# Converting most of the weights in pieces of 768 and 384 columns instead of three of 384

## The chip, the cores and the metric

One core of a Trainium2 chip. The metric is the device time of one execution in microseconds (us); of the kernel before there are three runs, 700.78 to 702.23, median 701.29. The profiled execution is a run of its own, with a time of its own.

## The reference

An attention-like recurrence feeds a bilinear feed-forward block. For each batch and head, a 48x48 state is multiplied by a complex number per row and takes in an outer product; then the feed-forward block runs on all 3072 tokens:

```python
mag = np.sqrt(a_re * a_re + a_im * a_im)
scale = np.minimum(mag, 0.999) / (mag + 1e-06)
a_re_n, a_im_n = (a_re * scale, a_im * scale)
for t in range(S):                      # S = 768, B = 4, H = 8, D = 48
    new_re = ar * S_re - ai * S_im
    new_im = ar * S_im + ai * S_re
    S_re, S_im = (new_re + kv, new_im)  # kv = outer(k[t], v[t])
    y[:, :, t] = einsum(q[t], S_re)
...
a = x @ w_a                             # 3072x384 by 384x1536
b = x @ w_b
return (a * b @ w_out)                  # 1536x384
```

The weights come as 64-bit floats. The kernel makes 32-bit ones of their two words itself.

## The kernel before

**Units.** The tokens are worked in 12 units (`NU`): two batches at a time, 128 time steps each, so 256 tokens. For each unit there are three kinds of work. `prep(u)` on VectorE (DVE), with logarithms, exponentials and squares on ScalarE (ACT), forms the running products of `a` and multiplies them into `q` and `k` (lines 178 to 192 scale `a`, L210 to L293 are the products, L308 the multiplication into tile `qk`). `stack(u)` copies `qk` by ten DMAs on SyncE's queue (SP), L345, into tile `stk`, one or two DMAs per head; it needs the last L308 of that unit. `attn(u)` on TensorE (PE) forms scores from `stk` (L378, four heads to a PSUM tile `pm`); DVE masks each tile (L381, tile `am`), four of these per unit; PE forms outputs (L418, tile `xp`), which ACT copies in two parts to `xh` (L422) and, after one correcting matmul (L426), `xl` (L429).

**Feed-forward.** For each unit 12 blocks `f` of 128 rows of the inner dimension follow: `gemm1` (18 matmuls L481 into tile `ab`), the product of its halves on ACT and DVE (L489 to L492), `gemm2` (6 matmuls L499). All matmuls of the feed-forward take a number as a high and a low part, so each weight is needed as a pair.

**Weights.** A block has 1152 weight columns: 384 of `w_a`, 384 of `w_b`, 384 of `w_out`. `load_weights` fetches them in three pieces of 384 columns (L124, 36 DMAs). `split_weights` converts a piece: three DVE operations (L133, L135, L137) put the 32-bit number together in a scratch tile `o_sb`; ACT rounds it to the high part (L141); PE forms the number minus its high part (L146, a matmul in two passes, and L147); ACT copies that to the low part (L148). The scratch tile is free again when L141 and L146 have read it. There are three of them, in the pool `moe`; two are also used at each unit's end for the output. Piece `w13` in the listings is piece 1 of block 3.

**Order.** Each engine runs its instructions in one fixed order. A scheduler makes it at build time, by its own idea of durations and free buffers; the source gives only the sequence of statements and some priorities (`MOE_FIRST`, `ATTN_FIRST`). The source asks for the first unit's `prep`, then six blocks of conversion, then the first `attn`; the other six blocks are converted during the first unit's feed-forward, one per block. The main loop runs `attn` one unit ahead and `prep` two or three.

Of the kernel before, what the change touches and what calls it, by code (L numbers as in the profile page):

```python
# [8 lines left out]
F32 = mybir.dt.float32  # L9
# [14 lines left out]
NJ = 3  # L24
# [18 lines left out]
KS = 2 * D  # L43
LAG = 2
HB = 3
O_BUFS = 3
CONV_ON_AB = 7
NCHK = NU * G + NU + 1
WPART = ((0, DM), (DM, DM), (2 * DM, DM))
CONV_FIRST = 6  # L50
P1_AT = 4
MOE_FIRST = 4000
# [14 lines left out]
def tile_kernel(ctx: ExitStack, tc: tile.TileContext, a_d, qk_d, v_d, w_d, qn_d, kn_d, vn_d, an_d, out_d):  # L67
# [51 lines left out]
        return ap.bitcast(F32R)  # L119

    def load_weights(f):
        for m, (c0, n) in enumerate(WPART):
            raws[f, m] = wpool.tile([128, n, 2], U32, name=f"w{m}{f}")
            sync.dma_start(out=raws[f, m].rearrange("p c s -> p (c s)"),  # L124
                           in_=w_d[f, :, c0:c0 + n].bitcast(U32))

    def split_weights():
        for f in range(NF):
            for m, (c0, n) in enumerate(WPART):
                raw = raws[f, m]  # L130
                t = moe.tile([128, n], F32, name="o_sb", bufs=O_BUFS)
                tu = t.bitcast(U32)
                vec.tensor_scalar(out=tu, in0=raw[:, :, 1], scalar1=3, scalar2=0x3FFFFFFF,  # L133
                                  op0=ALU.logical_shift_left, op1=ALU.bitwise_and)
                vec.scalar_tensor_tensor(out=tu, in0=raw[:, :, 0], scalar=29, in1=tu,  # L135
                                         op0=ALU.logical_shift_right, op1=ALU.bitwise_or)
                vec.scalar_tensor_tensor(out=tu, in0=raw[:, :, 1], scalar=0xC0000000, in1=tu,  # L137
                                         op0=ALU.bitwise_and, op1=ALU.bitwise_or)
                w_t[f, m] = wpool.tile([128, 2, n], F32, name=f"w{m}{f}")
                hi, lo = w_t[f, m][:, 0], w_t[f, m][:, 1]  # L140
                act.copy(out=r(hi), in_=t)  # L141
                if f < CONV_ON_AB:
                    lp = ps_ab.tile([128, 512], F32, name="ab")
                else:
                    lp = ps_m.tile([128, 512], F32, name="pm")
                pe.matmul(out=lp[:, 0:n], lhsT=ident, rhs=t, start=True, stop=False)  # L146
                pe.matmul(out=lp[:, 0:n], lhsT=r(nident), rhs=r(hi), start=False, stop=True)  # L147
                act.copy(out=r(lo), in_=lp[:, 0:n])  # L148
            yield


# [47 lines left out]
    def prep(u):  # L199
# [269 lines left out]


    def w_ab(f, part, blk):
        m, b = divmod(blk, NJ)
        return w_t[f, m][:, part, b * 128:(b + 1) * 128]

    def gemm1(f, xh, xl, ps_ab=ps_ab, moe=moe):
# [19 lines left out]
    def gemm2(f, hh, hl, os_):  # L495
        for tt in range(2):
            ts = slice(tt * 128, (tt + 1) * 128)
            for n, (ht, part) in enumerate(((hh, 0), (hh, 1), (hl, 0))):
                pe.matmul(out=os_[tt][:, 0:DM], lhsT=r(ht[:, ts]), rhs=r(w_t[f, 2][:, part, :]),  # L499
                          start=(f == 0 and n == 0), stop=(f == NF - 1 and n == 2))  # L500


# [128 lines left out]
    def second():  # L631
        w2, f2, hh, hl, os2 = pend.pop(0)
        gemm2(f2, hh, hl, os2)
        if f2 == NF - 1:
            for tt in range(2):
                o_sb = moe.tile([128, DM], F32, name="o_sb", bufs=O_BUFS)
# [118 lines left out]
```

## Time and profile before

| | |
|---|---|
| three runs | 700.78, 701.29, 702.23 us |
| profiled execution, its own time | 701.13 us |
| its span, first to last instruction | 699.4 us |
| PE busy | 656.8 us, 94% |
| DVE busy | 541.8 us, 77% |
| ACT busy | 320.2 us, 46% |
| weight DMAs (L124) | 36 of 384 KB, 8.1 us to landing |

The span is 1.7 us shorter than the profiled execution's time; that is what lies around it. A share is an average over the whole span: which engine the others wait for changes from one stage to the next, and has to be read from the stretch in question. A timeline row gives start, length, engine, line, operation, output<-input, and in brackets how long the engine sat idle before it and what ended that. A DVE instruction's length in such a row is longer than the step to the next one's start, since the end of one overlaps the beginning of the next; the steps are what adds up. "x2" merges equal neighbours.

### The profile page before, as it was taken

What the parts mean: (1) busy time and instruction counts of PE and PEld (TensorE: products, weight loads), DVE (VectorE), ACT (ScalarE), POOL (GpSimd) and SP (SyncE); (2) the same over time, 40 slices, a digit from 0 to 9 for tenths busy, and PEclk for the clock granted to TensorE, in tenths of its full rate; (3) what the DMA queues carried; (4) which work ended last, traced back from release to release, by engine and by line L of the source; (5) the groups of instructions that cost most, each with busy time, mean ns of one, the idle gap of its engine ahead of it and who ended that gap; (6) DMA issues with size and microseconds to landing.
All of it is one profiled execution on the core that took longest, in us unless ns stands there. A gap on an engine that the chain in (4) does not pass through costs nothing.

```text
span 699.4 us, 14330 instructions
## 1 busy us (share of the span) xinstructions
PE 656.8 (94%) x5862; PEld 612.5 (88%) x5862; DVE 541.8 (77%) x1239; ACT 320.2 (46%) x642; POOL 5.6 (1%) x11
## 2 busy tenths in 40 slices
PE   3547999999999999999999999999999999999996
PEld 1214889899899999999999999999998999999996
DVE  6999899998889989899898989989899353232221
ACT  6357755735546255462554646356434222222221
POOL 3000000000000000000000000000000000000000
PEclk9976999999999999999999999999999999999999
DMA  8963301513215033061431601520500500400000
GB/s 316 402 258 100 112 1 46 147 44 110 87 38 182 17 120 101 16 189 46 120 100 45 168 24 46 152 82 5 163 24 13 154 24 17 106 23 2 23 1 28
DMA packets 30232, 63.94 MB, mean 91 GB/s; under 512 B 3664, under 2 KB 7248, under 8 KB 30160
## 3 DMA queue, kind: packets, MB, share of 16 engines
q1 hardware_dynamic: 26704, 58.23, 26.4%
q10 hardware_dynamic: 3456, 4.72, 1.8%
q8 instruction: 48, 0.79, 0.5%
q14 instruction: 24, 0.20, 0.1%
HBM read 39.32 MB, written 4.72 MB: 63 GB/s over the span
## 4 chain that ended last, share of the span: by engine, by line
PE 50%; DVE 38%; ACT 5%; DMA 3%; issue 2%; SPq 1%; DVEq 0%; ACTq 0%
PE ab L481 23%; PE o L499 12%; PE xp L418 4%; DVE a_t L288 4%; PE pm L378 4%; DVE qk L308 3%; DVE pr L226 3%; DVE hl L492 3%; DVE h_t L490 2%; PE pm L437 2%; DVE z L293 2%; DVE pb L261 2%; DVE z L232 2%; DMA stk<-qk 2%; PE pm L146 2%
## 5 line engine op out<-in xcount | busy, mean ns | idle before, releaser
L481 PE MATMUL ab<-xh,w 128*128 128x256 f32 x1728 | 339.3, 285 | 0.0
L481 PEld LDWEIGHTS ab<-xh,w 128*128 128x128 f32 x1728 | 276.9, 189 | 2.0 <-issue 1.4
L481 PE MATMUL ab<-xl,w 128*128 128x256 f32 x864 | 244.8, 283 | 0.0
L481 PEld LDWEIGHTS ab<-xl,w 128*128 128x128 f32 x864 | 163.0, 189 | 0.4
L499 PE MATMUL o<-w,hh 128*128 128x384 f32 x576 | 152.9, 345 | 0.0
L490 DVE TENSOR_TENSOR h_t<-ab,h_t 128x256 f32<-128x256 f32 x144 | 60.4, 419 | 80.0 <-ACT h_t L489 79.6
L489 ACT COPY h_t<-ab 128x256 f32<-128x256 f32 x144 | 53.3, 370 | 150.1 <-PE ab L481 149.1
L499 PEld LDWEIGHTS o<-w,hh 128*128 128x128 f32 x576 | 97.0, 188 | 3.5 <-issue 2.8
L491 ACT CAST hh<-h_t 128x256 fp32r<-128x256 f32 x144 | 58.0, 403 | 90.2 <-DVE h_t L490 89.6
L499 PE MATMUL o<-w,hl 128*128 128x384 f32 x288 | 97.4, 338 | 0.0
L492 DVE TENSOR_TENSOR hl<-h_t,hh 128x256 fp32r<-128x256 f32 x144 | 60.5, 420 | 20.6 <-ACT hh L491 20.5
L146 PE MATMUL ab<-o_sb,ident 128*128 128x384 f32 x42 | 28.7, 784 | 29.1 <-DVE o_sb L137 29.1
L378 PE MATMUL pm<-stk 128*128 128x128 f32 x384 | 53.6, 279 | 2.3 <-DMA stk<-qk 2.3
L499 PEld LDWEIGHTS o<-w,hl 128*128 128x128 f32 x288 | 54.1, 188 | 0.2 <-issue 0.2
L378 PEld LDWEIGHTS pm<-stk 128*128 128x128 f32 x384 | 48.7, 192 | 6.1 <-issue 3.9
L226 DVE TENSOR_TENSOR pr<-z 128x384 f32<-128x384 f32 (+1 forms) x91 | 47.2, 525 | 4.2 <-ACT z L212 2.1
L288 DVE TENSOR_TENSOR a_t<-z,b_t 128x768 f32<-128x768 f32 x48 | 44.3, 952 | 0.1
L146 PEld LDWEIGHTS ab<-o_sb,ident 128*128 128x128 f32 x42 | 9.7, 274 | 39.2 <-DVE o_sb L137 29.5
L418 PE MATMUL xp<-am,v_t 128*32 128x128 f32 x768 | 41.4, 277 | 2.3 <-DVE am L381 2.0
L308 DVE TENSOR_TENSOR qk<-qk,z 128x1536 f32<-128x1536 f32 (+1 forms) x26 | 42.4, 1629 | 0.1
L381 DVE TENSOR_TENSOR am<-pm,mask 128x512 f32<-128x512 f32 x48 | 32.8, 685 | 6.1 <-PE pm L378 6.1
L437 PE MATMUL pm<-v_t,kt 128*96 128x96 f32 x320 | 34.6, 250 | 0.1
(105 smaller groups left out, 766.4 us busy)
## 6 DMA issues: line engine op xcount, KB each, us to landing
w<-in_dram SPq DMA_DIRECT2D x36, 384.0 KB, 8.1
qk<-in_dram SPq DMA_DIRECT2D x12, 768.0 KB, 4.9
stk<-qk SPq DMA_DIRECT2D x48, 192.0 KB, 3.3
a_t<-in_dram SPq DMA_DIRECT2D x11, 768.0 KB, 4.4
v_t<-in_dram SPq DMA_DIRECT2D x24, 256.0 KB, 2.7
stk<-qk SPq DMA_DIRECT2D x24, 192.8 KB, 3.1
out_dram<-o_sb ACTq DMA_DIRECT2D x24, 192.0 KB, 1.9
stk<-qk SPq DMA_DIRECT2D x16, 128.0 KB, 3.2
```

Of the source, the lines that this page charges most:

```text
L146: pe.matmul(out=lp[:, 0:n], lhsT=ident, rhs=t, start=True, stop=False)
L226: vec.tensor_tensor(out=pr[:, :, :, o:o + n], in0=view(zz, W + at_(i) + 2 * o, [[W, 2], [-W, 2], [2, n]]), in1=tok(slice(1, 3), i - 1, o, ...
L288: vec.tensor_tensor(out=pz[:, s].rearrange("p (j b e) -> p j b e", j=SUB // 2, e=2), in0=zb[:, 1 + s], in1=view(bb, (1 + k - s) * NB, [[0, ...
L308: vec.tensor_tensor(out=qk4[:, :, k, x0:x1], in0=qk4[:, :, 1, x0:x1], in1=z[:, k].rearrange("p (j t) -> p j t", j=NJ).unsqueeze(2).broadca ...
L378: pe.matmul(out=sp[:, h4], lhsT=stk[:, h, ks], rhs=stk[:, h, qs], start=True, stop=True)
L418: pe.matmul(out=xp[qd * 32:(qd + 1) * 32, ti], lhsT=l, rhs=rr, start=st, stop=sp_, tile_position=(0, qd * 32), skip_group_check=True)
L481: pe.matmul(out=ab[:, m * TOK:(m + 1) * TOK], lhsT=r(w_ab(f, part, m * NJ + i)), rhs=r(xt[:, i, :]), start=n == 0, stop=n == 8)
L489: act.copy(out=h_t, in_=ab[:, 0:TOK])
L490: vec.tensor_tensor(out=h_t, in0=ab[:, TOK:2 * TOK], in1=h_t, op=ALU.mult)
L491: act.copy(out=r(hh), in_=h_t)
L492: vec.tensor_tensor(out=r(hl), in0=h_t, in1=hh, op=ALU.subtract)
L499: pe.matmul(out=os_[tt][:, 0:DM], lhsT=r(ht[:, ts]), rhs=r(w_t[f, 2][:, part, :]), start=(f == 0 and n == 0), stop=(f == NF - 1 and n == 2))
```

## The change

From block 3 on, `w_a` and `w_b` of a block form one piece of 768 columns, and `w_out` stays a piece of 384. So nine blocks have two loads, two sets of three DVE operations and two L141 in place of three; L146, L147 and L148 still go by 384 columns, now two of each for a piece of 768. The scratch tiles are 768 wide, and there are two of them in place of three. A small scratch tile of the product chain (`pb`) has one buffer in place of two. Lines behind the edit have numbers 6 or 7 higher: L133, L135, L137 become L139, L141, L143; L308 becomes L315; L381 becomes L388; L212, L422, L429 become L219, L429, L436.

```diff
-O_BUFS = 3
+O_BUFS = 2
-WPART = ((0, DM), (DM, DM), (2 * DM, DM))
+def wpart(f):
+    return ((0, DM), (DM, DM), (2 * DM, DM)) if f < 3 else ((0, 2 * DM), (2 * DM, DM))
...
     def split_weights():
         for f in range(NF):
-            for m, (c0, n) in enumerate(WPART):
+            for m, (c0, n) in enumerate(wpart(f)):
                 raw = raws[f, m]
-                t = moe.tile([128, n], F32, name="o_sb", bufs=O_BUFS)
+                t = moe.tile([128, 2 * DM], F32, name="o_sb", bufs=O_BUFS)[:, 0:n]
...
                 act.copy(out=r(hi), in_=t)
-                if f < CONV_ON_AB:
-                    lp = ps_ab.tile([128, 512], F32, name="ab")
-                else:
-                    lp = ps_m.tile([128, 512], F32, name="pm")
-                pe.matmul(out=lp[:, 0:n], lhsT=ident, rhs=t, start=True, stop=False)
-                pe.matmul(out=lp[:, 0:n], lhsT=r(nident), rhs=r(hi), start=False, stop=True)
-                act.copy(out=r(lo), in_=lp[:, 0:n])
+                for o in range(0, n, DM):
+                    if f < CONV_ON_AB:
+                        lp = ps_ab.tile([128, 512], F32, name="ab")
+                    else:
+                        lp = ps_m.tile([128, 512], F32, name="pm")
+                    pe.matmul(out=lp[:, 0:DM], lhsT=ident, rhs=t[:, o:o + DM], start=True, stop=False)
+                    pe.matmul(out=lp[:, 0:DM], lhsT=r(nident), rhs=r(hi[:, o:o + DM]), start=False, stop=True)
+                    act.copy(out=r(lo[:, o:o + DM]), in_=lp[:, 0:DM])
...
-            pb = small.tile([128, 2, 2, G], F32, name="pb")
+            pb = small.tile([128, 2, 2, G], F32, name="pb", bufs=1)
```

The scheduler makes another order of it. **First place**, on DVE: the end of the first unit's `prep`, where the second L308 shown is the one that the first `stack` waits for. Before:

```order
L323 TENSOR_TENSOR qk_110<-qk_110,a_t_118 128x3x256
L137 SCALAR_TENSOR_TENSOR o_sb_502<-w25_162,o_sb_502 128x384
L308 TENSOR_TENSOR qk_110<-qk_110,z_117 128x3x256
L133 TENSOR_SCALAR o_sb_751<-w06_164 128x384
L308 TENSOR_TENSOR qk_110<-qk_110,z_117 128x3x256
L178 SCALAR_TENSOR_TENSOR a_t_118<-a_t_118 128x768
L135 SCALAR_TENSOR_TENSOR o_sb_751<-w06_164,o_sb_751 128x384
L133 TENSOR_SCALAR o_sb_761<-w16_166 128x384
L137 SCALAR_TENSOR_TENSOR o_sb_751<-w06_164,o_sb_751 128x384
L135 SCALAR_TENSOR_TENSOR o_sb_761<-w16_166,o_sb_761 128x384
L133 TENSOR_SCALAR o_sb_771<-w26_168 128x384
L137 SCALAR_TENSOR_TENSOR o_sb_761<-w16_166,o_sb_761 128x384
```

Now the same place, with the lines' new numbers; L388 is the first mask:

```order
L330 TENSOR_TENSOR qk_110<-qk_110,a_t_118 128x3x256
L139 TENSOR_SCALAR o_sb_770<-w07_162 128x768
L315 TENSOR_TENSOR qk_110<-qk_110,z_117 128x3x256
L141 SCALAR_TENSOR_TENSOR o_sb_770<-w07_162,o_sb_770 128x768
L315 TENSOR_TENSOR qk_110<-qk_110,z_117 128x3x256
L185 SCALAR_TENSOR_TENSOR a_t_118<-a_t_118 128x768
L143 SCALAR_TENSOR_TENSOR o_sb_770<-w07_162,o_sb_770 128x768
L139 TENSOR_SCALAR o_sb_784<-w17_164 128x384
L141 SCALAR_TENSOR_TENSOR o_sb_784<-w17_164,o_sb_784 128x384
L143 SCALAR_TENSOR_TENSOR o_sb_784<-w17_164,o_sb_784 128x384
L388 TENSOR_TENSOR am_483<-pm_478,mask_96 128x512
L192 TENSOR_TENSOR a_t_118<-a_t_118 128x768
```

Blocks are converted in their order, so the names tell how much is done: at the last multiplication six blocks and the first operation of block 6 before, seven blocks and two of three operations of the first piece of block 7 now. The first mask has 14 rows between it and that multiplication before (more than are shown), five now; at the fourth mask eight blocks are done in both.

**Second place**, on DVE: the first wide pieces, in the chain of small operations (L261, L267; now L268, L274) of the same `prep`. Before, the pieces w13, w23:

```order
L133 TENSOR_SCALAR o_sb_432<-w13_148 128x384
L261 TENSOR_TENSOR pb_282<-tt_264,b_t_269 128x24
L133 TENSOR_SCALAR o_sb_442<-w23_150 128x384
L267 TENSOR_TENSOR b_t_269<-pb_282 128x12
L135 SCALAR_TENSOR_TENSOR o_sb_432<-w13_148,o_sb_432 128x384
L261 TENSOR_TENSOR pb_285<-tt_264,b_t_269 128x24
L135 SCALAR_TENSOR_TENSOR o_sb_442<-w23_150,o_sb_442 128x384
L267 TENSOR_TENSOR b_t_269<-pb_285 128x12
L137 SCALAR_TENSOR_TENSOR o_sb_432<-w13_148,o_sb_432 128x384
```

Now, from the last operation of w03 (768 wide) to the first of w04, which takes the same one of the two scratch tiles:

```order
L143 SCALAR_TENSOR_TENSOR o_sb_404<-w03_146,o_sb_404 128x768
L274 TENSOR_TENSOR b_t_251<-pb_261 128x12
L141 SCALAR_TENSOR_TENSOR o_sb_418<-w13_148,o_sb_418 128x384
L268 TENSOR_TENSOR pb_264<-tt_246,b_t_251 128x24
L143 SCALAR_TENSOR_TENSOR o_sb_418<-w13_148,o_sb_418 128x384
L274 TENSOR_TENSOR b_t_251<-pb_264 128x12
L268 TENSOR_TENSOR pb_267<-tt_246,b_t_251 128x24
L274 TENSOR_TENSOR b_t_251<-pb_267 128x12
L139 TENSOR_SCALAR o_sb_428<-w04_150 128x768
```

Between the two wide pieces there are now seven other rows, two of them 384 wide.

**Third place**, on ACT: the copies at the end of the first `attn`. Before:

```order
L393 COPY kt_629<-pm_624 128x384
L422 CAST xh_512<-xp_587 128x3x128
L393 COPY kt_640<-pm_635 128x384
L212 ACTIVATE z_575<-z_575 128x768
L429 CAST xl_513<-xp_587 128x3x128
```

Now:

```order
L400 COPY kt_593<-pm_588 128x384
L219 ACTIVATE z_539<-z_539 128x768
L429 CAST xh_476<-xp_551 128x3x128
L400 COPY kt_604<-pm_599 128x384
L436 CAST xl_477<-xp_551 128x3x128
```

The 768-wide L212 stood between the last two copies and now stands ahead of the second `xh` copy.

More of the change, by code (lines that the diff above doesn't have):

```diff
@@ L128, in split_weights @@
         for f in range(NF):
-            for m, (c0, n) in enumerate(WPART):
+            for m, (c0, n) in enumerate(wpart(f)):
                 raw = raws[f, m]
-                t = moe.tile([128, n], F32, name="o_sb", bufs=O_BUFS)
+                t = moe.tile([128, 2 * DM], F32, name="o_sb", bufs=O_BUFS)[:, 0:n]
                 tu = t.bitcast(U32)
@@ L471, in w_ab @@
     def w_ab(f, part, blk):
-        m, b = divmod(blk, NJ)
+        m, b = divmod(blk, NJ) if f < 3 else (0, blk)
         return w_t[f, m][:, part, b * 128:(b + 1) * 128]
@@ L498, in gemm2 @@
             for n, (ht, part) in enumerate(((hh, 0), (hh, 1), (hl, 0))):
-                pe.matmul(out=os_[tt][:, 0:DM], lhsT=r(ht[:, ts]), rhs=r(w_t[f, 2][:, part, :]),
+                pe.matmul(out=os_[tt][:, 0:DM], lhsT=r(ht[:, ts]), rhs=r(w_t[f, len(wpart(f)) - 1][:, part, :]),
                           start=(f == 0 and n == 0), stop=(f == NF - 1 and n == 2))
@@ L635, in second @@
             for tt in range(2):
-                o_sb = moe.tile([128, DM], F32, name="o_sb", bufs=O_BUFS)
+                o_sb = moe.tile([128, 2 * DM], F32, name="o_sb", bufs=O_BUFS)[:, 0:DM]
                 with tc.high_priority(offset=MOE_FIRST):
```

## The prediction

> **What bounds the kernel now.** I read the 40 slices first, then the stretches of 20 us behind 80 us, then the totals of who PE waited for.
>
> ```profile
> PE   3547999999999999999999999999999999999996
> DVE  6999899998889989899898989989899353232221
> PEclk9976999999999999999999999999999999999999
> ```
>
> A slice is 17.5 us. In the first four PE is 30 to 70% busy and DVE 60 to 99%; from the fifth on PE is full. So there are two stages: one in which DVE sets the pace, to about 76 us, and a dense one to the end.
>
> ```profile
> core 0: us, PE busy (x) PEld busy (x) DVE busy (x) ACT busy (x) POOL busy (x), PEclk, DMA share, GB/s
> 680.00:700.00 20.00, 13.56 (x96) 12.95 (x94) 3.55 (x9) 4.08 (x10) 0.00 (x0) 0.96 0.08 25
> sum 620.00, PE 609.22 PEld 585.08 DVE 471.43 ACT 273.80 POOL 0.00; mean PE 19.65 PEld 18.87 DVE 15.21 ACT 8.83 POOL 0.00
> ```
>
> From 80 to 700 us PE is idle for 620 - 609.2 = 10.8 us, of which 20 - 13.6 = 6.4 us lie in the last slice, behind the last matmul. So 4.4 us of idle are all that the dense stage can give back.
>
> ```profile
> PE ab L146 <- DVE o_sb L137: 29.1, 13, 9.4
> PE pm L378 <- DMA stk<-qk: 2.3, 3, 1.5
> PE pm L389 <- DVE am L381: 1.0, 3, 0.5
> PE xp L418 <- DVE am L381: 0.5, 1, 0.5
> DVE o_sb L133 <- ACT w L141: 0.6, 1, 0.6
> ```
>
> PE's largest wait, 29.1 us, is for conversion in the first stage; but there PE's work is small, and what counts is when the dense stage begins. The three rows below it are from 80 us on: 2.3 us for the copies to `stk`, 1.5 for masks. DVE waited for a scratch tile once, 0.6 us. These rows of the timeline show how the first stage ends:
>
> ```profile
> 57.09 0.96 DVE L308 TENSOR_TENSOR qk<-qk,z 128x768 f32<-128x768 f32 x1
> 58.08 6.78 SPq L345 DMA_DIRECT2D stk<-qk  x10
> 61.62 0.76 PE L378 MATMUL pm<-stk 128*128 128x128 f32 x2
> 65.32 0.69 DVE L381 TENSOR_TENSOR am<-pm,mask 128x512 f32<-128x512 f32 x1
> 65.93 0.95 DVE L185 TENSOR_TENSOR a_t<-a_t 128x768 f32<-128x768 f32 x1
> 66.91 0.94 ACT L186 ACTIVATE a_t<-sc,biases 128x768 f32<-128x768 f32 x1
> 66.91 1.83 PE L378 MATMUL pm<-stk 128*128 128x128 f32 x14
> 69.46 0.68 DVE L381 TENSOR_TENSOR am<-pm,mask 128x512 f32<-128x512 f32 x1
> 70.93 0.68 DVE L381 TENSOR_TENSOR am<-pm,mask 128x512 f32<-128x512 f32 x1
> 72.40 0.68 DVE L381 TENSOR_TENSOR am<-pm,mask 128x512 f32<-128x512 f32 x1
> 75.25 0.44 PE L426 MATMUL xp<-xh,nident 128*128 128x384 f32 x1
> 75.46 0.86 ACT L212 ACTIVATE z<-z 128x768 f32<-128x768 f32 x1
> 76.21 0.48 ACT L429 CAST xl<-xp 128x384 fp32r<-128x384 f32 x1
> 76.33 0.61 PE L481 MATMUL ab<-xh,w 128*128 128x256 f32 x3
> ```
>
> The last L308 of the first unit ends at 58.05. At 58.08 the ten copies to `stk` start; they take 6.8 us to issue; the first score follows 3.5 us behind the first copy. Four masks later, at 76.33, `gemm1` begins. DVE spends the time between 58 and 72 us on conversion, for which nobody waits there. So the chain is: DVE's list up to the last L308, then the copies, the scores, the masks, the dense stage.
>
> **The change part by part.**
>
> *1. Fixed cost saved.* Steps from start to start on DVE:
>
> ```profile
> 9.99 0.35 DVE L133 TENSOR_SCALAR o_sb<-w 128x384 uint32<-128x384 uint32 x1
> 10.26 0.55 DVE L137 SCALAR_TENSOR_TENSOR o_sb<-w,o_sb 128x384 uint32<-128x384 uint32 x1
> 10.73 0.55 DVE L135 SCALAR_TENSOR_TENSOR o_sb<-w,o_sb 128x384 uint32<-128x384 uint32 x1
> 28.86 0.20 DVE L237 TENSOR_SCALAR z<-z 128x96 f32<-128x96 f32 x1
> 28.98 0.35 DVE L133 TENSOR_SCALAR o_sb<-w 128x384 uint32<-128x384 uint32 x1
> 42.44 0.96 DVE L293 TENSOR_TENSOR z<-a_t 128x768 f32<-128x768 f32 x1
> 43.31 0.36 DVE L133 TENSOR_SCALAR o_sb<-w 128x384 uint32<-128x384 uint32 x1
> ```
>
> At 384 columns L133 takes 0.27 and L135 and L137 0.47 each: a piece is 1.21 us. At 768 a two-input operation takes 0.87 (L293). For L133 at 768 no row stands: a one-input operation takes 0.12 at 96 columns and 0.27 at 384, which continues to 0.47; two of 384 would be 0.54, one at the two-input pace 0.87. I take 0.47. A wide piece is then 2.21 us, and a block 2.21 + 1.21 = 3.42 in place of 3 x 1.21 = 3.63. Nine blocks save 9 x 0.21 = 1.9 us of DVE.
>
> *2. What stands ahead of the last L308.* This is the largest term, and comes from the order (first place). Before, 18 pieces and one L133 stand there: 18 x 1.21 + 0.27 = 22.05 us. Now it is 13 narrow pieces (three blocks and w13 to w16), four wide ones (w03 to w06), and L139 and L141 of w07: 13 x 1.21 + 4 x 2.21 + 0.47 + 0.87 = 25.91 us. All else ahead of it is the same. DVE has no gap to take that: L308 ends 3.86 us later, and the copies to `stk` with it.
>
> *3. From there to the dense stage.* Before, 6 x 1.21 - 0.27 = 6.99 us of conversion run on DVE between L308 and the fourth mask, beside the copies. Now 0.87 + 1.21 = 2.08 us do, and then DVE waits for the scores. Does that make the stretch shorter? The fourth mask starts 72.40 - 58.05 = 14.35 us behind L308. The first needs the fourth head, 65.32 - 58.05 = 7.3 before; with no conversion among the score matmuls I take 6.9. In the new order L185, L188 and L190 follow it, with ACT's L186 between the first two: from 65.32 to 65.93, to 66.91, 0.94 for L186, 0.87 for each of the other two: 0.6 + 1.0 + 0.9 + 0.1 + 1.7 = 4.3, so the second mask starts at 11.2. A mask (0.6) and L192 (0.87), a mask and one L210 (0.87) follow: the fourth starts at 14.1, 0.2 earlier. A floor comes from the ten copies:
>
> ```profile
> L345 SPq DMA_DIRECT2D stk<-qk x10: 593/608/705, 58.1 to 64.3; - x10
> DMA to landing us min/median/max: 2.5/3.1/3.4
> ```
>
> The tenth is issued at 64.3 and lands some 3.1 us later, 9.3 us behind L308. So the second mask can't start ahead of 10.0, nor the fourth ahead of 12.9: 1.4 us earlier at most. On ACT (third place), L212 no longer holds up the last `xl` copy: L429 starts at 76.21 where its matmul, over at 75.69, would have let it start at some 75.75: 0.45 us earlier. The dense stage begins 3.86 - 0.2 - 0.45 = 3.2 us later (2.0 to 3.7).
>
> *4. Two scratch tiles for three.* A tile is free when PE has read it:
>
> ```profile
> 33.32 0.91 PE L146 MATMUL ab<-o_sb,ident 128*128 128x384 f32 x2 [0.51 <-DVE o_sb L137]
> 49.00 1.65 PE L146 MATMUL ab<-o_sb,ident 128*128 128x384 f32 x2 [4.70 <-DVE o_sb L137]
> ```
>
> That takes 0.9 us at the faster pace that the trace shows and 1.65 at the slower; a wide piece needs two, so 1.8 to 3.3. In the second place seven rows lie between w03's last operation and w04's first: 0.47 + 0.47, three of 0.085 and two of 0.105 us, together 1.4. So DVE waits there 0.4 to 1.9 us. Between w04 and w05 lie some 1.9 us: 0 to 1.4 more. From w05 to w06 there are 6 us, and from w06 to w07 3.5: nothing. The waits stand on DVE ahead of L308 and hold up all behind them, the copies and scores among it. PE was at its fast pace in that stretch before, so I take 1.0 of 0.4 to 3.3. The Trainium skill, "Perfetto Trace Analysis", section "Identifying Performance Opportunities", reads the same gap coming again on an engine that should be full as a hint of too little memory for the next tile. The trace of before has one such gap of 0.6 us.
>
> *5. The dense stage.* PE has the same matmuls. The shift of 3.2 + 1.0 = 4.2 us passes through, less what comes back. Before, twelve pieces were left to convert behind the fourth mask, 14.52 us; now four blocks, 13.68; and one L210 (0.87) is already done: DVE is 0.84 + 0.87 = 1.7 us less late than PE. One wait of PE can use that:
>
> ```profile
> 168.44 6.62 SPq L345 DMA_DIRECT2D stk<-qk  x10
> 171.93 0.46 PE L378 MATMUL pm<-stk 128*128 128x128 f32 x2 [1.49 <-DMA stk<-qk]
> ```
>
> The copies come when DVE is done, and 1.49 us of PE's idle time go. The later ones (4.4 in all with this) are small, and I leave them. *6. The rest costs nothing:* the loads (36 to 27) are spread over 40 us and one wait of 0.5 for them stands at the start, ahead of the wide pieces; `pb` is written and read by DVE alone, in order, so one tile orders nothing new; the output uses two scratch tiles a unit, 45 us apart. What SP has queued behind the copies (the next unit's loads of `qk`, `a`, `v`) starts late with them, beside a DVE list that is as late.
>
> Sum: 3.86 - 0.2 - 0.45 + 1.0 - 1.5 = +2.7 us. On the profiled execution, 701.13, that is 703.8; it lies 0.16 us under the median of the three runs, too little to matter.
>
> **The rivals.**
>
> *Faster (12%).* The saved 1.9 us of DVE decide: DVE sets the pace of the first stage, and PE is full afterwards, so the dense stage begins up to 1.9 us earlier: 699.2. Its condition is that the first scores don't wait for L308, or that DVE gains at least 3.9 us ahead of L308, so that the four operations added there are paid for. For it: DVE has no gaps from 20 to 64 us. Against it: the order, and that only four and a half of the nine blocks stand ahead of L308, worth 0.9 us. By the same page of the Trainium skill, section "Optimizing Scalar/DVE Operations", larger operations raise the throughput of a full engine, at about 60 ns for each one saved: by it 27 operations would give an estimated 1.6 us. The rows give 2 x 0.47 - 0.87 = 0.07 us each. [...]
>
> *No change (22%).* The dense stage takes back all: there are no waits for scratch tiles, so it begins 3.2 us late, and DVE's lead over PE serves not one wait but all on copies and masks, 2.3 + 1.5 = 3.8 us. That leaves between -0.6 us (all gone) and +1.4, so some 701.3. For it: these waits are all the idle time that PE has there. Against it: six of the seven are 0.5 us or so, units later, where DVE's list has again what it had before, and a lead of 1.7 us doesn't last.
>
> *Forecast, slower (66%).* 703.8. Its own range is 702.7 (no scratch waits, floor reached in step 3 in part) to 706.5 (2.3 more of scratch waits, or L139 at 768 as slow as 0.87: 5 x 0.4 = 2.0 more ahead of L308).
>
> **How the numbers follow.** About 0.2%, 1.4 us, is what a measurement can tell from no change. Slower by more, above 702.7: 66%; faster by more, below 699.9: 12%; between 22%. The range for 8 in 10 goes from 700.8, which takes in most of no change, to 706.6; left out are the faster case and the end at which all scratch waits are paid and nothing comes back (701.1 + 3.2 + 3.3 = 707.6).
>
> **What would show it.** Right: the copies of the first `stack` start at 62 to 65 us in place of 58.08; DVE idles some 3 us ahead of the first mask; L141 or L146 is named as what L139 waits for, 0.4 to 3 us in all; the first L481 at 79 to 82. Wrong: copies before 61, or the first L481 at 77 or earlier; then step 2 or 3 fails. If L481 is late by 4 but the time is not, step 5 does: look at PE's waits for `stk` and `am` behind 160 us. If a wide L139 steps by much more than 0.47, step 1 does.

## The result, and the profile after

The changed kernel takes 710.01 us (median of 4 runs, 709.07 to 711.59), the kernel before 701.76 us on the same chip: a ratio of 1.0109, 95% interval 1.0093 to 1.0124 (here and below the ratios are those on record for the runs, not quotients of the two medians, which would give 1.0118 here). It is slower, as forecast, but by 8 us, where 2.7 were forecast and 706.6 was the top of the range. The profiled execution after took 710.47 us (span 708.8), the one before 701.13 (span 699.4): 9.34 us to explain. One of the eleven runs of the version called halves below took 3554.86 us; its ratio leaves that run out, and its median would be 0.05 us lower without it.

The 40 slices of after, to be laid beside those of before:

```profile
PE   3664999999999999999999999999999999999996
DVE  6998699898989989899799989989889443223221
PEclk9985699999999999999999999999999999999999
```

The picture is the same, two stages. What is new lies in the first five slices: DVE has 8 and 6 in the fourth and fifth, where it had 9 and 8.

This is how the first stage of after ends (timeline; idle time and its releaser in brackets):

```profile
65.14 0.95 DVE L315 TENSOR_TENSOR qk<-qk,z 128x768 f32<-128x768 f32 x1
66.11 6.74 SPq L352 DMA_DIRECT2D stk<-qk  x10
69.74 2.12 PE L385 MATMUL pm<-stk 128*128 128x128 f32 x6 [4.92 <-DMA stk<-qk]
72.94 0.69 DVE L388 TENSOR_TENSOR am<-pm,mask 128x512 f32<-128x512 f32 x1 [3.66 <-PE pm L385]
74.69 3.36 PE L385 MATMUL pm<-stk 128*128 128x128 f32 x14
78.08 0.69 DVE L388 TENSOR_TENSOR am<-pm,mask 128x512 f32<-128x512 f32 x1 [0.64 <-PE pm L385]
79.56 0.68 DVE L388 TENSOR_TENSOR am<-pm,mask 128x512 f32<-128x512 f32 x1
80.25 2.08 PE L385 MATMUL pm<-stk 128*128 128x128 f32 x8
82.36 0.69 DVE L388 TENSOR_TENSOR am<-pm,mask 128x512 f32<-128x512 f32 x1 [1.26 <-PE pm L385]
85.45 0.44 PE L433 MATMUL xp<-xh,nident 128*128 128x384 f32 x1
85.93 0.48 ACT L436 CAST xl<-xp 128x384 fp32r<-128x384 f32 x1
87.00 0.37 PE L488 MATMUL ab<-xh,w 128*128 128x256 f32 x1
```

The copies to `stk` start at 66.11, 8.0 us behind the 58.08 of before, though the order accounts for 3.86 only. From the copies to the first `gemm1` (L488 here, L481 before) it is 20.89 us instead of 18.25, so `gemm1` is 10.7 us late. Fourteen score products take 3.36 us (before 1.83) and the last eight 2.08 (before 1.16), and both engines wait: PE 4.92 us for the copies, DVE 3.66 us for the first scores, 0.64 and 1.26 for later ones.

DVE's busy time in three stretches, up to the copies, to the first `gemm1`, and to the copies of the third `stack`, in before:

```profile
0.00:58.08 58.08, 51.08 (x143) 0.87 0.77 294
58.08:76.33 18.25, 15.93 (x28) 0.86 0.58 174
76.33:168.44 92.11, 87.14 (x204) 1.00 0.20 60
sum 168.44, DVE 154.14; mean DVE 51.38
```

and in after:

```profile
0.00:66.11 66.11, 56.06 (x141) 0.87 0.66 258
66.11:87.00 20.89, 13.81 (x21) 0.67 0.50 152
87.00:178.19 91.19, 84.29 (x186) 1.00 0.19 60
sum 178.19, DVE 154.16; mean DVE 51.39
```

The third `stack` comes 9.75 us later, at 178.19, with DVE busy for the same 154.2 us: up to there the whole loss is DVE's idle time, 24.0 us instead of 14.3. From there to the end it is 531.0 us before and 530.6 after. In a row, the length of the stretch is followed by the busy time, the number of instructions and the granted clock: 0.67 between copies and `gemm1`, where it was 0.86.

Where DVE idles ahead of the copies shows in the rows of a piece's first operation (L139) and of PE's reading products (L153) in after:

```profile
28.29 1.65 PE L153 MATMUL ab<-o_sb,ident 128*128 128x384 f32 x2 [2.19 <-DVE o_sb L143]
30.91 1.65 PE L153 MATMUL ab<-o_sb,ident 128*128 128x384 f32 x2 [0.65 <-DVE o_sb L143]
32.65 0.56 DVE L139 TENSOR_SCALAR o_sb<-w 128x768 uint32<-128x768 uint32 x1 [0.65 <-issue]
33.81 1.65 PE L153 MATMUL ab<-o_sb,ident 128*128 128x384 f32 x2 [0.94 <-DVE o_sb L143]
35.55 0.36 DVE L139 TENSOR_SCALAR o_sb<-w 128x384 uint32<-128x384 uint32 x1 [0.73 <-issue]
36.94 2.93 PE L153 MATMUL ab<-o_sb,ident 128*128 128x384 f32 x4 [1.17 <-DVE o_sb L143]
39.97 0.56 DVE L139 TENSOR_SCALAR o_sb<-w 128x768 uint32<-128x768 uint32 x1 [1.39 <-PE ab L153]
43.17 1.53 PE L153 MATMUL ab<-o_sb,ident 128*128 128x384 f32 x4 [1.41 <-DVE b_t L274]
```

Two of the three waits of L139 are put down to "issue", that is, to nothing that the profile shows. But each of the three ends 0.09 or 0.10 us behind PE's products for an earlier piece (30.91 + 1.65 = 32.56, 33.81 + 1.65 = 35.46, 36.94 + 2.93 = 39.87), so they are read here as waits for the tile that PE gives back; so is a fourth, of 0.33 us at 58.24 (56.50 + 1.65 = 58.15), for which the profile names ACT. Together they are 3.1 us.

In before, beside the row of 33.32 above:

```profile
28.99 1.65 PE L146 MATMUL ab<-o_sb,ident 128*128 128x384 f32 x2 [1.86 <-DVE o_sb L137]
30.90 1.65 PE L146 MATMUL ab<-o_sb,ident 128*128 128x384 f32 x2
34.24 0.81 PE L146 MATMUL ab<-o_sb,ident 128*128 128x384 f32 x2
36.41 0.91 PE L146 MATMUL ab<-o_sb,ident 128*128 128x384 f32 x2 [1.19 <-DVE o_sb L137]
```

In before PE has work almost without a break from 28.99 to 32.8, and from 33.32 to 40 us a piece takes it 0.91 us or less instead of 1.65. In after PE waits for DVE ahead of each of the pieces from 28.29 to 36.94 and takes 1.65 for a piece, 2.93 for two, while DVE waits for PE to free a tile: each holds the other up. From 36.94 PE works without a break to 41.77, and at 43.17 it is fast, 1.53 us for two pieces. By then only the wait of 0.33 us is still to come. From 20 to 62 us DVE was busy for 41.84 us before, 38.32 after:

```profile
20.00:62.00 42.00, 41.84 (x117) 0.77 0.70 263
```

```profile
20.00:62.00 42.00, 38.32 (x100) 0.83 0.61 245
```

The Trainium skill, "TensorE: Matmul & The Clock Gate", Part 1, says that TensorE's clock starts at half rate and rises only after some 3.4 us of sustained work. The trace agrees: the pace rises behind 3.8 us of nearly unbroken products in before and 4.8 in after, and not where gaps of 0.65 to 2.2 us stand between them. The length needed lies somewhat higher in these runs: stretches of 3.64 us, with gaps of 0.67 behind them, were not enough in the version with two narrow tiles (experiment 1). (The clock column reads 1.00 from 20 to 40 us in before and after, and 0.50 in that version, for pieces of the same 1.65 us, so here the durations tell, not the column.)

### The profile page after: what moved, and what is told of

Its sections match the earlier page's. It is cut to its first block, busy times and chain, and to the rows that moved or that the text cites. A ratio compares the mean times of both kernels' runs of the same rounds, so it can differ in the third digit from the quotient of the medians.

```text
span 708.8 us, 14301 instructions
## 1 busy us (share of the span) xinstructions
PE 658.2 (93%) x5862; PEld 611.3 (86%) x5862; DVE 541.7 (76%) x1212; ACT 317.4 (45%) x633; POOL 5.6 (1%) x11
## 4 chain that ended last, share of the span: by engine, by line
DVE 48%; PE 34%; DMA 8%; ACT 5%; issue 2%; SPq 2%; DVEq 0%; ACTq 0%
PE ab L488 13%; PE o L506 7%; DVE qk L315 5%; DVE a_t L295 5%; DVE pr L233 4%; DMA w<-in_dram 4%; DVE hl L499 4%; DVE h_t L497 4%; PE pm L385 3%; PE xp L425 3%; DVE z L239 3%; DVE z L300 2%; DMA stk<-qk 2%; DVE am L388 2%; DVE pb L268 2%
## 5 line engine op out<-in xcount | busy, mean ns | idle before, releaser
L488 PE MATMUL ab<-xh,w 128*128 128x256 f32 x1728 | 331.6, 282 | 0.0
L488 PEld LDWEIGHTS ab<-xh,w 128*128 128x128 f32 x1728 | 274.1, 188 | 1.8 <-issue 1.4
L488 PE MATMUL ab<-xl,w 128*128 128x256 f32 x864 | 241.6, 280 | 0.0
L488 PEld LDWEIGHTS ab<-xl,w 128*128 128x128 f32 x864 | 162.5, 188 | 0.3
L385 PE MATMUL pm<-stk 128*128 128x128 f32 x384 | 57.9, 293 | 8.2 <-DMA stk<-qk 7.5
L385 PEld LDWEIGHTS pm<-stk 128*128 128x128 f32 x384 | 51.6, 202 | 12.5 <-issue 8.7
L153 PE MATMUL ab<-o_sb,ident 128*128 128x384 f32 x42 | 30.2, 839 | 28.5 <-DVE o_sb L143 27.1
L153 PEld LDWEIGHTS ab<-o_sb,ident 128*128 128x128 f32 x42 | 10.9, 299 | 39.5 <-DVE o_sb L143 22.6
L315 DVE TENSOR_TENSOR qk<-qk,z 128x1536 f32<-128x1536 f32 (+1 forms) x26 | 42.4, 1630 | 0.1
L388 DVE TENSOR_TENSOR am<-pm,mask 128x512 f32<-128x512 f32 x48 | 32.8, 685 | 9.7 <-PE pm L385 9.6
```

Source lines behind the costliest of these rows:

```text
L315: vec.tensor_tensor(out=qk4[:, :, k, x0:x1], in0=qk4[:, :, 1, x0:x1], in1=z[:, k].rearrange("p (j t) -> p j t", j=NJ).unsqueeze(2).broadca ...
L385: pe.matmul(out=sp[:, h4], lhsT=stk[:, h, ks], rhs=stk[:, h, qs], start=True, stop=True)
L388: vec.tensor_tensor(out=am, in0=sp, in1=mask[:].unsqueeze(1).broadcast_to([128, 4, 128]), op=ALU.mult)
L488: pe.matmul(out=ab[:, m * TOK:(m + 1) * TOK], lhsT=r(w_ab(f, part, m * NJ + i)), rhs=r(xt[:, i, :]), start=n == 0, stop=n == 8)
```

## The experiments

Theory A: the order puts more conversion ahead of L308 (3.86 us), and two tiles make DVE wait on top of it. Theory B: wide pieces or two tiles cost by themselves, wherever the conversion stands. Theory C: what comes behind the copies is slow because PE has run empty. In the table, "ahead" is the conversion ahead of the last L308, worked out from the order and the steps of the prediction (for widths below 384, 0.07 us and the columns at the pace of 384); the copies, the first `gemm1` and the third `stack` are from each profile, medians and ratios to before (with their intervals) from the runs. The runs were made on several chips, on which before's median was 701.76 to 702.46, so the ratios are what compares.

| kernel | ahead, us | copies | gemm1 | third stack | median us | ratio |
|---|---|---|---|---|---|---|
| before | 22.05 | 58.08 | 76.33 | 168.44 | 701.76 | 1 |
| after | 25.91 | 66.11 | 87.00 | 178.19 | 710.01 | 1.0109 (1.0093 to 1.0124) |
| two narrow tiles | 22.05 | 61.82 | 80.02 | 174.34 | 706.72 | 1.0058 (1.0036 to 1.0081) |
| hold | 21.15 | 63.83 | 82.82 | 174.64 | 709.44 | 1.0103 (1.0077 to 1.0129) |
| warm scores | 25.91 | 66.40 | 85.83 | 176.94 | 711.71 | 1.0126 (1.0101 to 1.0152) |
| narrow operations | 22.52 | 61.37 | 80.44 | 175.28 | 702.76 | 1.0004 (0.9994 to 1.0013) |
| three wide tiles | 25.91 | 62.63 | 88.90 | 171.83 | 707.57 | 1.0077 (1.0062 to 1.0093) |
| fill | 24.10 | 61.60 | 79.97 | 171.48 | 703.79 | 1.0031 (1.0018 to 1.0044) |
| halves | 18.70 | 54.18 | 73.25 | 170.45 | 703.53 | 1.0019 (1.0009 to 1.0028) |
| thirds | 17.55 | 53.86 | 78.57 | 174.97 | 709.56 | 1.0110 (1.0094 to 1.0125) |
| fill and hold | 21.15 | 59.46 | 80.61 | 171.07 | 703.10 | 1.0015 (1.0004 to 1.0026) |
| before with fill | 21.78 | 57.56 | 77.13 | 168.82 | 704.30 | 1.0036 (1.0021 to 1.0051) |
| two narrow tiles, fill | 19.63 | 57.21 | 80.56 | 170.39 | 705.01 | 1.0040 (1.0026 to 1.0054) |

**1. Two narrow tiles.** On before:

```diff
-O_BUFS = 3
+O_BUFS = 2
```

> The kernel before, with two scratch tiles of 384 columns in place of three; its instructions ahead of the last L308 are the same (55 conversion operations, 22.05 us of DVE). Theory A (the change is late because of what the list puts ahead of L308, and the two tiles add waits on top): the copies of the first stack start at 58 to 61 us, 0 to 3 us behind the 58.08 of before, all of it waits of L133 for a tile that TensorE still reads; the time is 701 to 704 us. Theory B (the two tiles alone make the loss): the copies start 5 us or more late, and the time is 706 us or more.

The order ahead of L308 is that of before, and the copies come 3.74 us later, the time is 4.3 us longer (706.72 against 702.46 on that chip). The copies lie between A and B, the time is B's: the tiles cost more than A had it, though not all. From 20 to 62 us DVE is busy for 38.67 us, 3.2 less than in before:

```profile
20.00:62.00 42.00, 38.67 (x108) 0.50 0.65 251
```

PE's rows show the same list at the slow pace, where before reached 0.91 at 33.32:

```profile
30.74 1.65 PE L146 MATMUL ab<-o_sb,ident 128*128 128x384 f32 x2 [0.64 <-DVE o_sb L137]
33.44 1.65 PE L146 MATMUL ab<-o_sb,ident 128*128 128x384 f32 x2 [0.74 <-DVE o_sb L137]
37.75 1.65 PE L146 MATMUL ab<-o_sb,ident 128*128 128x384 f32 x2 [0.67 <-DVE o_sb L137]
```

So one tile fewer, with no other change in the source, costs about half of what the change costs.

**2. Hold.** On after; it adds seven small copies:

```diff
+HOLD = 6
...
+                if f >= HOLD:
+                    vec.tensor_copy(out=t[:, 0:1], in_=gate)
```

> The changed kernel, with one more column beside the biases: DVE writes it when the first unit's second head is ready, and the conversion of the first column of blocks 6 and later reads nothing before it, so that 45 conversion operations (21.15 us) stand ahead of the last L308 in place of 53 (25.91), and 11 (4.97 us) in place of 4 (2.08) between it and the fourth mask. It adds seven copies of one column that compute nothing. Wide pieces, two scratch tiles and all loads stay. Theory A (order): the copies start 4.8 us or more ahead of the 66.11 of after, at 58 to 61 us, the first gemm1 (L488 of after) starts by 80, and the time is 702 to 705 us. Theory B (wide pieces or the two tiles cost as such, wherever they stand): the copies may move, the time stays within 1.5 us of after's, 708.5 to 711. If the waits for tiles gather in the part that is left, it lies between.

4.76 us of conversion went from ahead of L308, but the copies came only 2.3 us earlier: DVE is now busy for only 36.59 of the 42 us from 20 to 62. The waits for tiles are still there (3.3 us at the conversion), and a gap of the chain that conversion had filled stays empty (1.8 us, in which DVE waits for ACT). The first `gemm1` is 4.2 us earlier and the third `stack` 3.6, yet the ratio can't be told from after's. A's time (702 to 705) failed; alone, this run settles nothing.

**3. Warm scores.** On after, behind the first unit's `prep`:

```diff
+    dp = ps_o.tile([128, 512], F32, name="o0")
+    for n in range(4):
+        pe.matmul(out=dp[:, 0:384], lhsT=ident, rhs=qk[:, 0, 0, 128:512], start=True, stop=True)
```

> The changed kernel, with four TensorE products of 128x128 by 128x384 added behind the first unit's last L308, whose result nothing reads; the order of all else is that of after. In after, TensorE was idle for 4.92 us ahead of the scores at 69.74, and its granted clock stood at 0.50 in the stretch behind. Theory C (the scores are late because TensorE had run empty): the copies start at 66 as in after, the granted clock in the stretch from 70 to 80 us is above 0.7, the first gemm1 starts at 84 to 86 in place of 87.00, and the time is 707.5 to 709 us. If the clock doesn't matter, the time is that of after within 0.5 us, and if the added products stand in the way of the scores, it is up to 2 us longer.

Part of C holds: from copies to `gemm1` it takes 19.43 us instead of 20.89, and the granted clock in that stretch is 0.82 instead of 0.67. Only the last eight score products became faster (1.16 us instead of 2.08); the fourteen ahead of them still take 3.36. The time shows nothing of it, and C's time (707.5 to 709) failed. In this profile the third `stack` is 1.25 us earlier than in after, and the end 1.4 later. A place where it was lost is a wait of PE for masks in the dense stage, behind which the granted clock is low; after has no stretch of 5 us like it (windows; PE's busy time is the second number):

```profile
535.00:540.00 5.00, 3.48 (x26) 2.98 (x26) 4.62 (x20) 1.36 (x3) 0.00 (x0) 0.96 0.00 0
540.00:545.00 5.00, 5.00 (x80) 4.58 (x79) 4.80 (x13) 0.78 (x2) 0.00 (x0) 0.70 0.00 0
```

**4. Narrow operations.** On after, with its wide loads, tiles and casts:

```diff
+                for p in [slice(o, o + DM) for o in range(0, n, DM)]:
+                    vec.tensor_scalar(out=tu[:, p], in0=raw[:, p, 1], scalar1=3, scalar2=0x3FFFFFFF,
+                                      op0=ALU.logical_shift_left, op1=ALU.bitwise_and)
...
```

> The changed kernel with its wide loads, its two wide scratch tiles and its wide casts, but with the three DVE operations of a wide piece done as two times three of 384 columns. 56 conversion operations (22.52 us) stand ahead of the last L308 in place of 53 (25.91), and 13 (5.11 us) in place of 4 between it and the fourth mask. Theory A (the width of an operation counts, since the list puts a like number of operations into the gaps of the first unit's chain): the copies start 3.4 us or more ahead of after's 66.11, at 60 to 63 us, and the time is 703 to 706.5 us. Theory B (the two wide tiles, held until TensorE has read all of them): the time stays at 708.5 to 711 us. Theory C (the fixed cost saved matters): it is longer than after's, above 711.

The time is that of before again, a little less than A had expected: B falls as far as wide loads and wide tiles go, and so does the fixed cost (the C that was named for this run). With two tiles of 768 columns, what loses is the wide operation; two tiles of 384 lost 4.3 us without one. (Its profiled execution, 705.38 us, lies 2.6 above its median and waits 1.7 us for a load, so its columns in the table stand higher than usual.) How much of this is the order (22.52 us ahead instead of 25.91) and how much that the first half of a tile can go to PE while DVE converts the second, this run doesn't tell. Nor does the whole gain lie where A puts it. The third `stack` is 6.8 us behind before's, an estimated 4.2 if the surplus of 2.6 lies all ahead of it; so 5.5 of after's 9.75 us are gained up to there. The rest comes behind it: from there to the end it takes 528.2 us instead of 531.0, in units that the edit reorders too.

**5. Three wide tiles.** On after; the room comes from buffers of the dense stage:

```diff
-O_BUFS = 2
+O_BUFS = 3
-HB = 3
+HB = 2
...
-            t = vpool.tile([128, 512], F32, name="v_t")
+            t = vpool.tile([128, 512], F32, name="v_t", bufs=1)
```

> The changed kernel with three scratch tiles of 768 columns in place of two; to make room, the dense stage has two buffers for three of hh and hl and one for two of v_t, so that its time behind the first gemm1 is not to be compared, only what comes ahead. The conversion ahead of the last L308 is that of after, 25.91 us, 3.86 more than before. Theory A (order and waits for tiles add up): DVE's waits for a tile between 20 and 60 us, 3.6 us in after, fall below 1 us, and the copies of the first stack start at 62 to 63 us, 3.5 to 4.5 behind before's 58.08 and as much ahead of after's 66.11. Theory D (the order costs nothing, since DVE would have waited in those places anyway, and the tiles cost all): the copies start at 58 to 60. Theory E (the tiles cost nothing): they stay at 65 to 66.

A holds. DVE is busy for 41.27 of the 42 us, and the copies start 4.55 us behind before's, 3.86 of which are the order's, and 3.48 ahead of after's:

```profile
20.00:62.00 42.00, 41.27 (x106) 0.58 0.60 243
```

```profile
61.64 0.96 DVE L315 TENSOR_TENSOR qk<-qk,z 128x768 f32<-128x768 f32 x1
62.63 6.74 SPq L352 DMA_DIRECT2D stk<-qk  x10
```

PE is slow here too, 1.65 us for a piece up to 35 us, and first 0.81 at 38.76: with three tiles DVE hardly waits even for the slow pace. The first `gemm1` is later than in after (88.90) because PE waits 1.71 us, at 85.10, for `v_t`, which has one buffer here.

**6. Fill.** On after, behind each conversion of blocks 1 to 6:

```diff
+                if 0 < f < CONV_ON_AB:
+                    dp = ps_o.tile([128, 512], F32, name="o0")
+                    for d in range(2):
+                        pe.matmul(out=dp[:, 0:DM], lhsT=ident, rhs=hi[:, 0:DM], start=True, stop=True)
```

> The changed kernel, with two TensorE products of 128x128 by 128x384 added behind each conversion of blocks 1 to 6, whose result nothing reads. They give TensorE work between the pieces, where it was idle. 24.1 us of conversion stand ahead of the last L308 here, 1.8 less than in after. Theory F (with two tiles DVE and TensorE wait for each other, TensorE never works long enough in one stretch to reach its faster pace, and the waits are those of the slow pace): the conversion products (L153) take 0.9 us in place of 1.65 from some 30 us on, DVE's waits for a tile fall from 3.6 to below 1.5 us, and the copies start at 60 to 62.5 us. If the pace isn't what makes the waits, or the added products hold up the conversion's, the copies start at 64 to 67. The time follows the first gemm1, 622 to 624 us behind it.

F holds. PE's products for a piece take 0.8 to 0.9 us from 24 to 45 us, where most took 1.65 in after, and DVE is busy for 41.26 of 42 us with the same two tiles:

```profile
28.42 0.91 PE L153 MATMUL ab<-o_sb,ident 128*128 128x384 f32 x2 [1.77 <-DVE o_sb L143]
33.26 0.87 PE L153 MATMUL ab<-o_sb,ident 128*128 128x384 f32 x2
```

```profile
20.00:62.00 42.00, 41.26 (x104) 0.90 0.63 251
```

The copies come 4.5 us earlier than in after (1.8 of it from the order, which the added products move), `gemm1` 7.0, and the ratio falls from 1.0109 to 1.0031, some 5.5 us. Fourteen score products take 1.83 us again. Work that nobody reads made the changed kernel faster by keeping PE at work; where it still idled, for 4.83 us up to 50.79, the next piece took 1.62.

**7 and 8. Halves and thirds.** On before, for blocks 3 to 7, pieces in twos of 192 columns or threes of 128 (`DM // 3`):

```diff
+                for p in [slice(o, o + DM // 2) for o in range(0, DM, DM // 2)] if 3 <= f < 8 else (slice(0, DM),):
```

> The kernel before, with the DVE operations of blocks 3 to 7 done in twos of 192 columns; tiles, loads and casts are those of before. It adds 45 operations, at about 0.07 us of fixed cost each 3.2 us of DVE. 60 conversion operations (an estimated 18.7 us) stand ahead of the last L308 in place of 55 (22.05), and 41 (9.7 us) in place of 17 (7.0) between it and the fourth mask. Theory A (a like number of operations goes into the gaps of the first unit's chain, so that their size sets when it ends): the copies start at 54.5 to 56 us, ahead of the 58.08 of before, the first gemm1 (L481 of before) 1 to 3.5 us earlier than 76.33, and the time is 698.5 to 701, faster than before though DVE has more to do. If the fixed cost decides: the time is 702 to 705.

> As the kernel with blocks 3 to 7 in twos of 192 columns, but in threes of 128: 90 operations more than before, 6.3 us of fixed cost. 64 conversion operations (an estimated 17.6 us) stand ahead of the last L308, and 69 (12.5 us) between it and the fourth mask. Theory A: the copies start at 53.5 to 55.5 us; but 12.5 us of conversion in the 14.35 us between L308 and the fourth mask hold up the masks, so the first gemm1 is at 73 to 76 and the time 698.5 to 702. If the fixed cost decides: above 704.

The order's half of A holds again, now the other way: 3.35 us less conversion ahead of L308 bring the copies 3.9 us forward in the halves, and the first `gemm1` 3.1:

```profile
54.18 6.73 SPq L346 DMA_DIRECT2D stk<-qk  x10
73.25 0.36 PE L482 MATMUL ab<-xh,w 128*128 128x256 f32 x1
```

But the time is not shorter; it is 1.5 us longer in the halves (703.53 against 702.06) and 7.5 in the thirds. A's times failed, and both times lie where the rival, that the fixed cost decides, had put them. The sum row of DVE up to the halves' third `stack` tells why:

```profile
sum 170.45, DVE 156.39; mean DVE 52.13
```

It is idle for 14.06 us, like before's 14.30, and busy for 2.25 us more: the third `stack` is 2.0 us late. In the thirds DVE is busy for 159.66 us, 5.5 more, and idle for 15.31; the third `stack` is 6.5 late. To that point DVE's whole list sets the pace, not the time at which the first scores start. What was not converted ahead of L308 is missing later: at 122 to 125 us PE has waited for a piece of the last blocks, 2.0 us in the halves and 2.3 in the thirds, where it didn't wait in before, and the granted clock is 0.69 from 120 to 125 us in the halves and 0.66 from 125 to 130 in the thirds. How much of the loss is this and how much the added work, these runs don't tell.

**9. Fill and hold** together, on after.

> The changed kernel with both: two TensorE products that nothing reads behind each conversion of blocks 1 to 6, and conversion of blocks 6 and later held until the first unit's second head is ready, so that 21.15 us of it stand ahead of the last L308 (25.91 in after, 22.05 in before) and 4.97 behind, to the fourth mask. If the loss is what DVE idles up to the copies of the third stack (24.0 us of 178.2 in after, 14.3 of 168.4 in before, with the same busy time of 154.2), by waits for tiles at TensorE's slow pace and by waits for scores with nothing to convert beside them, then both go: copies of the first stack at 58.5 to 61, DVE idle 14 to 16.5 us up to the third stack, which starts at 168 to 171, and the time is 700.5 to 703. If held-back conversion leaves gaps in DVE's list that nothing fills (in the version with the hold alone the copies came at 63.83 although 0.9 us less conversion than in before stood ahead), the copies come at 61 or later and the time is 703 to 706.

Of after's 8 us more than 7 are gone, by 703.10 against before's 702.37 on that chip. The copies (59.46) came as expected; the third `stack` (171.07), DVE's idle time up to it (16.54 us) and the time lie just above what was expected, 0.1 us or less.

**10 and 11. Fill without the change:** the same products on before, and on before with two tiles.

> The kernel before (three narrow tiles) with two TensorE products that nothing reads behind each conversion of blocks 1 to 6; 21.78 us of conversion ahead of the last L308 in place of 22.05. DVE waited for a tile once there, 0.6 us. If TensorE's slow pace costs only where there are two tiles, the time is that of before within 1 us, 701 to 703, copies at 57 to 58.5. If the slow pace costs before's scores and casts too (they start 14.35 us behind L308 with DVE idle 1.5 us at masks), it is up to 2 us less, 699.5 to 701. If the added products stand in the way, it is 703 or more.

> The kernel before with two narrow scratch tiles (which alone gave 706.72 us, copies at 61.82) and two TensorE products that nothing reads behind each conversion of blocks 1 to 6. 19.63 us of conversion stand ahead of the last L308 in place of 22.05. Theory F (two tiles make DVE and TensorE wait for each other at TensorE's slow pace): the conversion products take 0.9 us from 30 us on, DVE's waits for a tile between 20 and 60 us fall from 4.6 to below 1.5 us, copies at 56 to 58.5, time 701.5 to 704. If two tiles cost by their number alone: waits 3 us or more, time 705 to 707.

Before becomes 1.9 us longer, as expected for products that stand in the way. But the third `stack` is only 0.4 us later; the rest is lost behind it (533.0 us to the end instead of 531.0), where none of the added products runs (the last one ends at 74.3), and why is open. With two narrow tiles the copies come at 57.21 instead of 61.82, as F had it, but `gemm1` stands later in PE's order and 1.7 us of the time is all that comes back; F's time failed. Among the three kernels with fill the ratios are 1.0036 (three narrow tiles), 1.0040 (two) and 1.0031 (the change): with PE kept at work, tiles and pieces no longer make a difference that these runs can tell, though the order still differs (24.10 us ahead with the change, 21.78 and 19.63 without). No version beat before; the halves and the thirds, which were to, lost.

## Why the prediction was wrong

The direction was right, with the forecast's mechanism in it; the sum was 6.6 us short on the profiled execution. By its own steps:

*Step 1 held.* The groups of conversion by shape in after:

```profile
L141 DVE SCALAR_TENSOR_TENSOR o_sb<-w,o_sb 128x384 uint32<-128x384 uint32 x18 | 10.0, 556 | 0.2
L141 DVE SCALAR_TENSOR_TENSOR o_sb<-w,o_sb 128x768 uint32<-128x768 uint32 x9 | 8.6, 959 | 0.0
L139 DVE TENSOR_SCALAR o_sb<-w 128x384 uint32<-128x384 uint32 x18 | 6.4, 356 | 1.8 <-issue 1.0 <-ACT w L147 0.3 <-ACT a_t L311 0.3
L139 DVE TENSOR_SCALAR o_sb<-w 128x768 uint32<-128x768 uint32 x9 | 5.0, 560 | 2.3 <-PE ab L153 1.4 <-issue 0.7 <-PE pm L153 0.3
```

Between 384 and 768 columns L139 grows by 0.20 us (assumed 0.20) and L141 by 0.40 (assumed 0.40).

*Step 2 held:* +3.86 was forecast, and three wide tiles, with 0.7 us of DVE's idle time left from 20 to 62 us, gave 4.55.

*Step 4 is the term of the sum that was mis-sized.* "PE was at its fast pace in that stretch before, so I take 1.0 of 0.4 to 3.3." The copies are 8.03 us late, 3.86 of it order, so this step cost 4.17 as the remainder, or 3.48 as what a third wide tile gives back. The waits themselves, 3.1 us, came from the slow end of the prediction's own 0.4 to 3.3. The error is in carrying PE's pace over: it was fast in before because the third tile let two pieces queue up for it; the same list with two narrow tiles stays at 1.65 us for a piece (experiment 1). In after PE became fast at 43 us, when the waits but for 0.33 were over. The waits also stood on narrow pieces (0.73 at 35.55), which share the two tiles, where only wide ones had been counted; and a wait costs a little more than its length, since neighbouring operations on DVE no longer overlap: some 0.09 us at each. That explains less than half of the 1.12 us by which busy time up to the copies rose beyond the 3.86 of added work (4.98 in all); the rest is open.

*Step 3 failed in sign.* Forecast -0.65 in all, measured 20.89 - 18.25 = +2.64. The first mask came as forecast, 72.94 - 66.09 = 6.85 us behind the end of L315 ("I take 6.9"). What failed is the next part: the second and the fourth mask were placed by DVE's and ACT's operations alone, at 11.2 and 14.1, as if every score came in time. They came at 11.99 and 16.27, since DVE waited for scores at both (0.64 and 1.26 us). The conversion products that were gone had kept PE at work; without them it idled for 4.92 us and took 3.36 us for fourteen scores instead of 1.83, and 2.08 for eight instead of 1.16. The four added products of experiment 3 brought back 1.5 us, and with the fill this stretch took 18.37 us, about as long as in before. The ACT term, -0.45, failed too. L436 starts as its product ends (85.89, 85.93), as forecast, but the first `gemm1` doesn't wait for that copy: in before it starts at 76.33, ahead of the copy's end at 76.69. From the fourth mask to `gemm1` it took 4.64 us instead of 3.93, with four products of L396 now ahead of it on PE. The range for this step had only gains in it.

*Step 5 was right by 0.2 us for the wrong reason.* 10.67 us at `gemm1` became 9.4 at the end, 1.3 given back (1.5 forecast). But the wait that was to vanish is still there:

```profile
178.19 6.62 SPq L352 DMA_DIRECT2D stk<-qk  x10
181.58 0.46 PE L385 MATMUL pm<-stk 128*128 128x128 f32 x2 [1.56 <-DMA stk<-qk]
```

The stretch from `gemm1` to the third `stack` is 0.92 us shorter, with 2.85 us less of DVE's work in it (84.29 and 87.14). DVE had no lead to give: with idle time of 9.7 us more behind it, its list was as late as PE's. That the amount is right is luck.

*Step 6 held where the trace shows it:* ahead of the rows that use `pb` (L268, L274) DVE has no idle time that a profile counts, and behind 20 us no wait for a load is named.

The sum with measured terms: 3.86 + 4.17 + 2.64 - 1.3 = 9.4, against 9.34 measured; as 4.17 is a remainder, this shows where the time went and proves nothing more. The upper bound named in the prediction, 707.6, had the order and the tiles at their worst, and still the gain of 0.65 from step 3. Of the signs named, DVE's wait ahead of the first mask came (3.66 us for some 3), while the copies (66.11) and the first `gemm1` (87.00) lie beyond the 62 to 65 and 79 to 82 us given for them.

*The rivals.* "No change" and "faster" fell. The condition of "no change", no waits for tiles and PE's waits for copies and masks gone, didn't hold (3.1 us, and 1.56 at one copy alone). That of "faster", that DVE's saved time decides, was right in part: DVE's list does set the pace, even to the third `stack`, but the saving of 1.9 us doesn't show (154.14 and 154.16 busy), and idle time is what changed. What happens behind the third `stack` stays open: every edit reorders the later units too, and from the third `stack` to the end the profiles of the table, leaving out the kernel with fewer buffers, take 528 to 533.5 us.

## What to carry to other kernels

Before making operations wider, look at what they fill: a scheduler that drops one into each gap of a dependency chain puts more work ahead of the chain's end (25.91 us for 22.05 here), and leaves less to fill the gaps behind it (2.08 for 6.99). When a buffer is taken from a producer and a consumer that feed each other, price the wait at the consumer's slowest pace in the trace, since the fast one may exist only thanks to the buffer. And add up the busy and idle time of the engine that sets the pace, up to the last point at which others wait for its whole list, here the third `stack`; in the halves and the thirds an earlier milestone that didn't shorten that sum gained nothing.

## What was not expected of the hardware

Products of one piece took PE 1.65 us or 0.81 to 0.91 at the same shape, by how steadily it had worked before; gaps of 0.65 to 2.2 us between pieces were enough for the slow pace, 1.8 times the time and more. Unbroken work of 3.64 us was not enough for the fast one in one version, and 3.8 us was in another. Keeping it busy with products that nobody reads brought the changed kernel from a ratio of 1.0109 to 1.0031. The pace was also lost in the dense stage, in three of the profiles: behind some 1.5 us of idle time, at a granted clock of 0.70 over the next 5 us (warm scores), and at waits of 2.0 and 2.3 us for a piece, at 0.69 and 0.66 over 5 us (halves and thirds).
